# Cross network on one core: the searched run of row products is carried on to the row-major layer

## The chip, the cores and the metric

One core of a Trainium2 chip. The time is device microseconds (us) of one execution, median of several runs. A profile is one execution, in microseconds from the start of its span.

## What is computed

```
B, F, D, L = 16384, 26, 16, 6          # Din = F * D = 416
x = x0                                 # x0 [B, Din], ws [L, Din, Din], bs [L, Din], bf16
for l in range(L):
    proj = einsum('bd,de->be', x, ws[l]) + bs[l]
    x = x0 * proj + x
return x
```

## The kernel before

**Tiling.** The 16384 rows are eight groups g of 2048, and a job (g, l) is layer l of one group. All jobs but the last hold x transposed: features on partitions, rows along the free axis. 416 features are three blocks of 128 and a tail of 32. A tile (g, l, i) is the output block i of a job for its 2048 rows; it has four chunks j of 512 rows, and a chunk is one PSUM bank. A chunk sums 13 products over 32 input features each: 12 with `wm` (L1040) and one with the tail rows of the weights, `w3` (L1044). Such a row product uses one quarter of TensorE's rows, a strip, so four of them run side by side. Below, a *slot* is the time of one row product on each of the four strips. A chunk is 3.25 slots.

**The stream.** `stream` (L1005) emits most of the kernel's products. The order is a searched table, `ORDER`: each letter names a strip and how many chunks ago the chunk that it serves was begun, and stands for that chunk's 3 products on that strip, or 4 where the strip also holds its tail rows. The function `replay` turns letters into (time, strip, chunk, bank) by its own estimates; the instructions then go out in that order, with semaphores for what they really need. A bar `|` is an *event*: the strips stop and `tails` computes the 32 tail outputs of a batch of jobs, as 128x32 products (L697) and 32x32 corners (L685). Before, the stream runs from tile (0,2,1) to the tail rows of tile (7,4,0), with 14 events of three jobs.

**What follows a chunk.** ScalarE adds the bias and writes it from PSUM into `tw` (L550); for each pair of chunks VectorE multiplies by x0 (L562) and adds x (L567). Each add is held back until the next multiply is queued, or the tile ends. VectorE runs its instructions strictly in the order they were added. The tails of a batch go the same way with `ts`: the batch's job number 1 comes first, by VectorE straight from PSUM (L604), then the others by ScalarE (L608); multiply L610, add L612.

**Rotations.** For groups with `turn_of(g, 1)` above zero, the tail outputs of odd and even layers sit on different strips. `prefill`, called in `tails` when the batch is done, then copies the new tail of a job, rotated by some strips, into the buffer of the next tail: two DMAs on SyncE's queue (L444, L445). The add L612 of that job's *next* event adds into this buffer, so it waits for both DMAs. Groups 6 and 7 have such rotations.

**Outputs.** When the sixth layer of a group has its three tiles and its tail, `output(g)` puts on SyncE's queue a transpose of block 0 (L880), of the tail (L888), of blocks 1 and 2 (L880), and a store of the group (L916) that waits for them all. All go through one buffer `ost`. In `tails` this happens job by job in the batch's order, so the output of group 5, whose job (5,5) is the first of the 14th batch, stands on the queue ahead of the rotations of that batch's other two jobs.

**The end.** After the stream come, with whole 128-row products: (7,4,0) (L650), (6,5,0), (6,5,1), the last batch of tails (7,4) and (6,5), then (6,5,2) as 128x32 columns (L638), (7,4,1), (7,4,2), whose tail rows are L671 and L665. A job `FR` does whole products and then rows, `RF` the reverse, so that two jobs share one change of mode. The last job (7,5) is computed row-major for the output: for each kk of four, tail rows (L1171) and bias (L1176) by strips, whole products (L1130) into four banks, then ScalarE (L1182), VectorE multiply (L1188) and add (L1194), store (L1201). It needs x of (7,5), the outputs of the tiles (7,4,i), as weights (L1130, block by block) and row-major as `x5n`: block 0 and 1 by transposes on SyncE (`rest_turn`, L928), block 2 by TensorE (`turn_last`, L1141, copied by L1150), the tail by L1155 and L1163. The output of group 6 goes through `ost` as well; its transposes need the store of group 5 to have read `ost`.

Of the kernel before, what the change touches and what calls it, by code (L numbers as in the profile page):

```python
# [21 lines left out]
class Program:  # L22
# [182 lines left out]
    "ABCDAJCXaFTMWDUNSLYBKTMZjGANDaMpCPUJCXIROEDBaTUJCITVCQLVCAXNaALVaQHNKUTBQKDRICbRK|AJDWQJDCfUNSDM"  # L205
    "dSbJECbURCTINWDUJSPAJCTAZSPUJCDVYOTJAaDYVKTENCbNUSDJAXSYJGPAVODNUDOJUTCIRCDUNSbAJTaMVKHQBCXQNCPI"
    "ZSDJQCDMVaTEJOXBUDOAZXOIRGDYBSXARLOYBXKMZG|QBPSIVDCPAZOXQJGDQBaTINCLAdSXJYOHRACTNUCPJUSDAVCXRMaL"
    "FUCXARWPYBKPAdaLUNCLMVTCNISDcBWPIRCLAVSbMBKPYVSHMB|CTMVCPIVCDUNaTIBaTVAKTNUGDMVSDINCXYJCDMVSbIFW"
    "PQBCTMVCPIVSDIBWTANKTYVODAZOTUJGDURODINCbUJODBMSbIVCTUBSPIVGDQVCTMJWDAZSXINGDUBSXIBKTAZKPcRGAZPW"
    "QBP|QBOLRECTBCUPZSAPRaXASJPUBKUDVSAPRKAbSNcDOUbFKDURKDIRCbQJOXBIODVAOTUJCLQVCDUNSbEJWDQVCTINCbUJ"  # L210
    "ODIBaTVAKTNUGDMVSDINCXBcXSNAKPAZWLAVKTYNGDYNSDYN|ICXJTACVQPCNAPeVAPeRYLWNQDKNbCIBWTYBSLMVCLMVCXM"
    "JSDAdWPQBLOQBbKNQCDdMWTZEODNUKTABOXAVCTcVOLERCDcRaPAJWbMRKHYBCXQNCPIZSDJQCDMVaDMJSbAJTOYVGDMVCjU"
    "N|ISDJTAKRMDJCQDNeITVGMbBWIDRWIDRKAbJSMDBObQJCDdOQXJaMDJWMTBKAXhSMDJOUDVKQPFCMDBaQfVKALRWMDJOUDV"
    "KATBOYjREWDROULBKUTBSIBLCUdCMLZSAbJSUDRKMXeFLQBCXMR|CPISFDQCTIBaDUZKDQJWbMBXOIZCLQBSbIdODIVCTUJO"
    "DIVODIBbCNYXKERDCUdTaIBTaJUOHAVCTMVKDUJSDAVCXQNKDYJWfAJWTMZGDMVCXcNS|IDJTECRCTANaDYVKTMFWDUBOXAN"
    "KXZQODZATOJUCLURODINCbIBWTJYOHAVCTMVKDUJSDIRDCUNSbBISbVAKPURCLMRWDINCXIBWTJgOHAVCTMVKDUJSDAVCXQN"
    "KDYJSfAJaPURGDMdCbUN|ISDJTECRCTANaDMVKTFYWDAVOTYJGXAVODNUDOJUTCIRODIBSbUJPCIVDQCZTMBaLMBaXIBWLQZ"
    "ODIZCXQZKPAJWDRMWDNUKTBISBDUORbAOZDaULNQGXJCQXBAWPRaIDRKUDJSUPGBAbVCMDVOYLFSUPBeMXRCM|RCPISFDQCT"
    "IBaTIVOHQBPCMVDOAZWPBUOLQBCfURODIdWPQZGDQNCbINWDINXGQBPAWBQPKVDIVSPAJODYJCXQKZPEBWDQNWLAVKTAJSAD"
    "OVYDNKTYBKbMVSHBeMXRCM|RCPISFDQCDMVaTIBSbUBTKMVCLMVSDIBSXIZDKURDSMJCbIBSXIZOHQBCTMVCPIVSDQJCTIBa"  # L220
    "DUZSLAJbQOVHAOBbUOBLUChTIVOALVOQDJCXQBiLMSVDKMBbWJMHCVASXdIDJSUPCJUDSVIDSBMbRCMLRCcbJOALVMaDJMaD"
    "JYOXRAO|ANXKQBLSABOXYRGLMVDWNACbNQWDNISDJAWfBcSXJMGbVQCPRCPISFDAeTUBKTMVCLUNSDMJTCIBWTIdOHQBPCMV"
    "DOAZWPBUKDQVCfIRWPYFCXQZCPIRWDJQWPEBCTAZSPUJCLAZCXMRaLUBWLAVLSgNXGIRCDUNS|IDJTAKRMDJCQbJWATVCQPJ"
    "WALBaUTBODUadTIGVATVOIDJWAXRKYPFCMDBaMTCZMLRWALRCAfROUDJeUTaBQPKVEDVSMDJOAfJCQXKZMDJWATJWMDVKMTB"
    "CARaXMBKPZUDWRIPaAJbCYVTO|EJDWQBPCNAbOVLQCJDUiRLaAJbSUNDKMXCBMTWJYHOAVPCMVDOUBPWIRDIORXENKLAUKBN"
    "CD"
# [3 lines left out]
def replay(tails, events, needs, keep, part):  # L230
# [12 lines left out]
    size = [[(3 if c < n - keep else part) + (r == tails[c]) for r in range(4)] for c in range(n)]  # L243
# [62 lines left out]
def bass_standalone__cross_network_dcn__recsys_kernel(  # L306
# [21 lines left out]
    order[-6:] = [(5, 5), (7, 3), (6, 4), (7, 4), (6, 5), (7, 5)]  # L328
# [209 lines left out]
    def evacuate_chunk(g, l, i, j, b, read):  # L538
# [35 lines left out]
        if len(out_) == NJ:  # L574
            todo.append(lambda: finish_tile(g, l))
# [50 lines left out]
    HALVES = ((1, 2), (2, 1), (3, 0))  # L626
    halves = [63]

    def full(g, l, i, banks, first, chunk_major, after_chunk=None, chunks=range(NJ), ts_=range(NT), columns=False):
# [4 lines left out]
        for t, j in seq:  # L634
            if columns:
                for c in range(NJ):
                    o = slice(c * T32, (c + 1) * T32)
                    add("pe", lambda h, t=t, j=j, c=c, o=o: h.matmul(  # L638
                        psum[o, banks[j] * CH:(banks[j] + 1) * CH],
                        wm[l][:, t, i * P + c * T32:i * P + (c + 1) * T32], src(t, j, j + 1),  # L640
                        start=(first and t == 0), stop=(not first and t == NT - 1), tile_position=(0, c * T32)),
                        reads=[stok(t, j), wm_tok(l, i)], writes=[("ps", banks[j])])
                continue
            n = 1
            if (g, l) in HALVES and halves[0] and t != (0 if first else NT - 1):
                halves[0] -= 1
                n = 2
            w = CH // n
            for k in range(n):
                add("pe", lambda h, t=t, j=j, k=k, w=w: h.matmul(  # L650
                    bank(banks[j])[:, k * w:(k + 1) * w], wm[l][:, t, ecols], src(t, j, j + 1)[:, k * w:(k + 1) * w],
                    start=(first and t == 0), stop=(not first and t == NT - 1)),
                    reads=[stok(t, j), wm_tok(l, i)], writes=[("ps", banks[j])])
            if after_chunk and t == NT - 1:
                after_chunk(j)
# [21 lines left out]
    def tails(batch, corners_last=False, banks=None):  # L677
# [198 lines left out]
    def output(g):  # L876

        s, s3 = xset[(g, L)], xtail[(g, L)]
        def turn(t, j0=0, j1=NJ):
            add("sp", lambda h: h.dma_start_transpose(  # L880
                ost[:, j0 * KK:j1 * KK, t * P:(t + 1) * P], xs[s][:, t * GC + j0 * CH:t * GC + j1 * CH]),
                reads=[("x", s, t, j) for j in range(j0, j1)], writes=[("ost", t, j) for j in range(j0, j1)],
                lane="ot" if g < LAST - 1 else f"ot_{t}{j0}", batch=g)

        turn(0)
        if g == LAST - 1:
            turn(1)
        add("sp", lambda h: h.dma_start_transpose(ot3[:, :, :], x3s[s3][:, :]),  # L888
            reads=[("x3", s3)], writes=["ot3"], lane="ot3", batch=g)
        if g < LAST - 1:  # L890
            spread("pool")
# [3 lines left out]
        else:  # L895
            turn(2, 0, 2)
            turn(2, 2, NJ)
        free_x.append(s)
        free_3.append(s3)

# [35 lines left out]
    behind = ("tile", (LAST, L - 2), 0)  # L936
# [3 lines left out]
    tiles += [(jb, i) for jb in order[3:-1] for i in range(NT)]  # L940
# [4 lines left out]

    for i in range(1, NT):
        late = items.index(("tile", (LAST, L - 2), i))
        items.append(items.pop(late))
# [4 lines left out]
    while k < len(items):  # L953
# [8 lines left out]
        else:  # L962
            single = 1 if items[k] == behind else single + 1
# [25 lines left out]
    for n, it in enumerate(items):  # L989
        if it == behind:  # L990
            prev = None
# [11 lines left out]
    mode[len(items) - 1] = "RF"  # L1003

    def stream(run, keep, part):  # L1005
# [10 lines left out]
        needs = [[(t, place[(g, l - 1), t]) for t in range(NT if c < len(chunks) - keep else part)  # L1016
                  if c - place.get(((g, l - 1), t), -99) < 30] for c, ((g, l), i, j) in enumerate(chunks)]
        plan, read, left = replay([quad(g, l, j)[0] for (g, l), i, j in chunks], [len(b) for n, b in due],
                                  needs, keep, part)
# [4 lines left out]
        count, seen = {}, {}  # L1024
        for _, r, c, b in plan:
            if r < 0:
                dve[0] = max(dve[0], phases.pop(0)) + PAIR * len(behind_tail) + TAILS
                tails(due.pop(0)[1], corners_last=True, banks=c)
                continue
# [9 lines left out]
            if t < (NT if c < len(chunks) - keep else part):  # L1039
# [9 lines left out]
        home = {c: b for _, r, c, b in plan if r >= 0}  # L1049
        ring[:] = sorted(left)  # L1050
        (g, l), i, _ = chunks[-1]
        banks = [home[c] for c in range(len(chunks) - keep, len(chunks))]
        if (g, l + 1) not in xset:
            xset[(g, l + 1)] = free_x.pop(0)
# [22 lines left out]
    s_lo, s_hi = items.index(("tile", (0, 2), 1)), items.index(behind) + 1  # L1077
    for n, it in enumerate(items):
        if n == s_lo:
            stream(items[s_lo:s_hi], NJ, 0)  # L1080
        if s_lo <= n < s_hi - 1:
            continue
# [11 lines left out]
        if n == s_hi - 1:  # L1094
            pass
        elif mode[n] in ("FR", "F1"):
            banks = job_banks()
            full(g, l, i, banks, True, False, columns=items[n - 1][0] == "tails")
            rows32(g, l, i, banks, False, mode[n] == "F1")
            evacuate(g, l, i, banks, list(range(NJ)), 2)  # L1100
        else:
            banks = job_banks()
            rows32(g, l, i, banks, True)
            if n == len(items) - 1:
                full(g, l, i, banks, False, True, lambda j: evacuate(g, l, i, banks, [j], 1))
            else:
                full(g, l, i, banks, False, False)
                evacuate(g, l, i, banks, list(range(NJ)), 2)
        finish_tile(g, l)
        if (g, l) == (LAST, L - 2) and i < NT - 1:  # L1110
            if i:
                spread("act")
            rest_turn(i)


# [6 lines left out]

    def x3col(j, kk):
        return s3[quad(g, l, j)[1], kk * P:(kk + 1) * P]
# [43 lines left out]
    def nat_rows(kk, bks, first=True, begun=()):  # L1168
        for j in range(NJ):
            r, q = quad(g, l, j)  # L1170
            add("pe", lambda h, j=j, q=q, r=r: h.matmul(  # L1171
# [107 lines left out]
```

## Time and profile before

| what | us |
|---|---|
| median of 3 runs (lowest, highest) | 467.52 (467.04, 468.06) |
| span of the profiled execution, first to last instruction | 465.7 |
| what lies around the span, by the median | 1.8 |
| TensorE busy | 458.9 (99%) |
| VectorE busy | 404.2 (87%) |
| ScalarE busy | 379.1 (81%) |

The profiled execution's own time outside its span is not recorded, so the 1.8 us is the median less the span. The engines' busy shares are averages over stages with different limits; the stages at the end have to be read from the rows of the timeline. A row of the timeline has its start, its length, the engine (PE TensorE, DVE VectorE, ACT ScalarE, SPq SyncE's queue of DMAs), the line, the operation and its operands.

### The profile page before, as it was taken

Reading aid. Unit: us, or ns where it says so; the run is one execution under the profiler, and the core shown is the slowest. Engines: PE = TensorE matmul, PEld = TensorE weight load, DVE = VectorE, ACT = ScalarE, POOL = GpSimd, SP = SyncE. Lnnn points to the kernel's source line nnn. Section 1 sums busy time; section 2 is a strip of 40 time slices with the busy share of each in tenths; the row PEclk is TensorE's granted clock in tenths of the full one; section 3 lists DMA queues with packets and bytes.
Section 4 is the critical chain, followed back from the end, with each engine's and each line's share of the span. In section 5 each row is a group of like instructions: output and inputs, shape, how many; then the busy total and the mean of one; then the engine's idle time right before and its main releaser. Section 6 shows DMA issues by size and latency. Waiting matters only on the chain.

```text
span 465.7 us, 17469 instructions
## 1 busy us (share of the span) xinstructions
PE 458.9 (99%) x7827; PEld 263.8 (57%) x7833; DVE 404.2 (87%) x700; ACT 379.1 (81%) x608; POOL 6.8 (1%) x15
## 2 busy tenths in 40 slices
PE   9999999999999999999999999999999999999995
PEld 5444566555556677555655556565575566755442
DVE  2887998989989899979989898888989889898897
ACT  4687888788888888888878888788887887889785
POOL 1000000000000000000000000000000000000000
PEclk9999999999999999999999999999999999999998
DMA  8986949101002978084858437990100095027899
GB/s 229 185 177 144 160 113 190 29 3 26 1 4 38 158 210 155 22 141 149 149 92 154 145 78 141 160 296 23 25 2 4 25 148 172 14 49 169 183 161 292
DMA packets 139087, 53.77 MB, mean 115 GB/s; under 512 B 112762, under 2 KB 138500, under 8 KB 139012
## 3 DMA queue, kind: packets, MB, share of 16 engines
q1 hardware_dynamic: 138856, 52.54, 52.5%
q8 instruction: 61, 1.00, 0.9%
q10 hardware_dynamic: 156, 0.11, 0.1%
q14 instruction: 14, 0.11, 0.1%
HBM read 5.97 MB, written 13.63 MB: 42 GB/s over the span
## 4 chain that ended last, share of the span: by engine, by line
PE 93%; DVE 4%; DMA 1%; issue 1%; ACT 0%; SPq 0%; DVEq 0%
PE ps L1040 70%; PE ps L697 7%; PE ps L1044 6%; PE ps L650 6%; PE ps L638 2%; PE ps L685 1%; DMA wm<-in_ws_dram 1%; DVE x L1194 1%; DVE x L1188 1%; DVE x L528 1%; DVE tw L523 1%; PE ps L671 1%; ACT tw L514 0%; PE ps L789 0%; SPq L734 0%
## 5 line engine op out<-in xcount | busy, mean ns | idle before, releaser
L1040 PE MATMUL ps<-x,wm 32*128 32x512 bf16 x6000 | 356.0, 374 | 0.0
L550 ACT ACTIVATE tw<-ps,bias 128x512 bf16<-128x512 f32 x500 | 310.5, 688 | 46.4 <-PE ps L1040 35.9
L1040 PEld LDWEIGHTS ps<-x,wm 32*128 32x128 bf16 x6000 | 212.5, 92 | 127.7 <-ACT tw L550 4.1
L562 DVE TENSOR_TENSOR tw<-tw,x 128x1024 bf16<-128x1024 bf16 x250 | 168.2, 689 | 39.6 <-ACT tw L550 38.9
L567 DVE TENSOR_TENSOR x<-tw,x 128x1024 bf16<-128x1024 bf16 x250 | 163.5, 690 | 0.3
L1044 PE MATMUL ps<-x,w 32*128 32x512 bf16 x504 | 151.7, 374 | 0.0
L1044 PEld LDWEIGHTS ps<-x,w 32*128 32x128 bf16 x504 | 42.7, 92 | 6.6
L514 ACT ACTIVATE tw<-ps,bias 128x512 bf16<-128x512 f32 (+1 forms) x46 | 35.0, 839 | 12.0 <-PE ps L671 7.9
L650 PE MATMUL ps<-x,wm 128*128 128x512 bf16 x146 | 33.6, 379 | 1.0 <-issue 0.8
L697 PE MATMUL ps<-x,wm 128*32 128x512 bf16 x564 | 33.6, 380 | 0.0
L608 ACT ACTIVATE ts<-ps,bias 128x512 bf16<-128x512 f32 x33 | 21.0, 687 | 14.7 <-PE ps L685 14.7
L523 DVE TENSOR_TENSOR tw<-tw,x 128x1024 bf16<-128x1024 bf16 (+1 forms) x35 | 21.4, 627 | 4.9 <-ACT tw L514 4.7
L650 PEld LDWEIGHTS ps<-x,wm 128*128 128x128 bf16 x152 | 13.9, 98 | 19.0 <-issue 3.2
L697 PEld LDWEIGHTS ps<-x,wm 128*32 128x32 bf16 x564 | 13.5, 96 | 18.7 <-ACT tw L550 4.7
L528 DVE TENSOR_TENSOR x<-tw,x 128x1024 bf16<-128x1024 bf16 (+1 forms) x35 | 20.6, 624 | 0.0
L612 DVE TENSOR_TENSOR x<-ts,x 128x512 bf16<-128x512 bf16 x47 | 18.4, 420 | 0.4
L610 DVE TENSOR_TENSOR ts<-ts,x 128x512 bf16<-128x512 bf16 x33 | 13.0, 418 | 0.0
L604 DVE SCALAR_TENSOR_TENSOR ts<-ps,bias,x 128x512 bf16<-128x512 f32 x14 | 10.5, 748 | 2.2 <-PE ps L685 2.2
L909 POOL COPY ost<-ot 128x512 bf16<-128x512 bf16 x6 | 5.3, 890 | 411.3 <-DMA ot<-x 411.3
L1130 PE MATMUL ps<-wm,x 128*128 128x416 bf16 x48 | 9.8, 340 | 0.1
L1182 ACT ACTIVATE x<-ps 128x416 bf16<-128x416 f32 x16 | 7.6, 518 | 2.4 <-PE ps L1130 2.4
L799 DVE COPY x<-ps 128x512 bf16<-128x512 bf16 x5 | 2.0, 423 | 8.5 <-PE ps L789 8.5
(50 smaller groups left out, 76.9 us busy)
## 6 DMA issues: line engine op xcount, KB each, us to landing
out_dram<-ost SPq DMA_DIRECT2D x6, 1664.0 KB, 7.1
x<-x SPq DMA_DIRECT2D x24, 96.0 KB, 2.3
x<-in_x_dram SPq DMA_DIRECT2D x8, 208.0 KB, 4.4
x<-in_x_dram SPq DMA_DIRECT2D x4, 416.0 KB, 8.0
out_dram<-ost SPq DMA_DIRECT2D x2, 832.0 KB, 6.0
wm<-in_ws_dram SPq DMA_DIRECT2D x5, 312.0 KB, 3.4
x<-x SPq DMA_DIRECT2D x22, 64.0 KB, 2.0
out_dram<-x SPq DMA_DIRECT2D x3, 416.0 KB, 4.8
```

The source lines that it names most:

```text
L514: add("act", lambda h, a=a, w=w, b0=b0: h.activation(tw[r][:, a * CH:(a + w) * CH], psum[:, b0 * CH:(b0 + w) * CH], ACT_F.Identity, bias=b ...
L523: add("dve", lambda h, a=a, e=e: h.tensor_tensor(tw[r][:, a * CH:e * CH], tw[r][:, a * CH:e * CH], x0s[s0][:, i * GC + a * CH:i * GC + e * ...
L528: add("dve", lambda h, a=a, e=e: h.tensor_tensor(xs[so][:, i * GC + a * CH:i * GC + e * CH], tw[r][:, a * CH:e * CH], src(i, a, e), ALU.ad ...
L550: add("act", lambda h: h.activation(tw[r][:, j * CH:(j + 1) * CH], bank(b), ACT_F.Identity, bias=bias[:, i, l:l + 1], scale=1.0), reads=[( ...
L562: add("dve", lambda h: h.tensor_tensor(tw[r][:, o], tw[r][:, o], x0s[s0][:, c], ALU.mult), reads=[("tw", r, k) for k in both] + [x0_tok(s0 ...
L567: add("dve", lambda h: h.tensor_tensor(xs[so][:, c], tw[r][:, o], src(i, a, a + 2), ALU.add), reads=[("tw", r, k) for k in both] + [stok(i ...
L608: add("act", lambda h: h.activation(ts[r][:, :], bank(b), ACT_F.Identity, bias=bias[:, 3, l:l + 1], scale=1.0), reads=[("ps", b), "bias"], ...
L612: add("dve", lambda h: h.tensor_tensor(x3s[so][:, :], ts[r][:, :], res, ALU.add), reads=[("ts", r)] + rtok, writes=[("x3", so), ("x3", so, ...
L650: add("pe", lambda h, t=t, j=j, k=k, w=w: h.matmul(bank(banks[j])[:, k * w:(k + 1) * w], wm[l][:, t, ecols], src(t, j, j + 1)[:, k * w:(k ...
L697: add("pe", lambda h, t=t, j=j, src=src, l=l, b=b, ro=ro, qo=qo: h.matmul(psum[qo, b * CH:(b + 1) * CH], wm[l][:, t, NT * P:D], src(t, j, ...
L1040: add("pe", lambda h, l=l, t=t, j=j, b=b, q=q, ecols=ecols, src=src, kw=kw: h.matmul(bank(b), wm[l][q, t, ecols], src(t, j, j + 1)[q, :], ...
L1044: add("pe", lambda h, l=l, b=b, q=q, ecols=ecols, s3=s3, kw=kw: h.matmul(bank(b), w3[l][q, ecols], s3[q, :], **kw), reads=tok3 + [("w3", l ...
```

## The change

The stream runs to the last tile, (7,4,2), and has 15 events; its last four entries are the tail-row and bias products of the row-major layer's kk = 0 (two products for each chunk, on one strip). `stream` returns the banks of these four and the four free ones. The table `ORDER` is new from its first letter. The last jobs are reordered: (6,4) before (7,3), and the tiles of (6,5) and (7,4) are mixed. The 14th batch is now (5,5), (6,4), (7,3) and the 15th (6,5), (7,4). The whole products after the stream, the modes of the last items and `HALVES` go. The transposes of group 6's output are emitted tile by tile as its tiles finish, those of (7,4) likewise, and the transpose of group 6's tail with its batch.

```diff
-def replay(tails, events, needs, keep, part):
+def replay(tails, events, needs, keep):
-    size = [[(3 if c < n - keep else part) + (r == tails[c]) for r in range(4)] for c in range(n)]
+    size = [[3 + (r == tails[c]) if c < n - keep else 2 * (r == tails[c]) for r in range(4)] for c in range(n)]
...
-    order[-6:] = [(5, 5), (7, 3), (6, 4), (7, 4), (6, 5), (7, 5)]
+    order[-6:] = [(5, 5), (6, 4), (7, 3), (6, 5), (7, 4), (7, 5)]
...
         for g, l in batch:
+            if (g, l) == (LAST - 1, L - 1):
+                turn_rest(g)
             if corners_last:
                 prefill(g, l + 1)
...
+    def turn_rest(g):
+        s3 = xtail[(g, L)]
+        add("sp", lambda h: h.dma_start_transpose(ot3[:, :, :], x3s[s3][:, :]),
+            reads=[("x3", s3)], writes=["ot3"], lane="ot3", batch=g)
+
+    def turn_out(g, t):
+        s = xset[(g, L)]
+        for j0, j1 in ((0, NJ),) if t < NT - 1 else ((0, 2), (2, NJ)):
+            add("sp", lambda h, j0=j0, j1=j1: h.dma_start_transpose(
+                ost[:, j0 * KK:j1 * KK, t * P:(t + 1) * P], xs[s][:, t * GC + j0 * CH:t * GC + j1 * CH]),
+                reads=[("x", s, t, j) for j in range(j0, j1)], writes=[("ost", t, j) for j in range(j0, j1)],
+                lane=f"ot_{t}{j0}", batch=g)
...
-    tiles += [(jb, i) for jb in order[3:-1] for i in range(NT)]
+    tiles += [(jb, i) for jb in order[3:-3] for i in range(NT)]
+    end6, end7 = order[-3:-1]
+    tiles += [(end6, 0), (end6, 1), (end7, 0), (end6, 2), (end7, 1), (end7, 2)]
...
-    def finish_tile(g, l, n=1):
+    def finish_tile(g, l, n=1, i=0):
         tiles_done[(g, l)] = tiles_done.get((g, l), 0) + n
+        if (g, l) == (LAST - 1, L - 1):
+            turn_out(g, i)
+        elif (g, l) == (LAST, L - 2) and i < NT - 1:
+            if i:
+                spread("act")
+            rest_turn(i)
...
+    def nat_row(kk, j, b, first):
+        r, q = quad(LAST, L - 1, j)
+        s3, tok3 = x3_src(LAST, L - 1)
+        add("pe", lambda h: h.matmul(
+            bank(b, n=D), s3[q, kk * P:(kk + 1) * P], w3[L - 1][q, :], start=first, stop=False, tile_position=(r * T32, 0)),
+            reads=tok3 + [("w3", L - 1, r)], writes=[("ps", b)], row=r)
...
+            if c >= len(chunks):
+                j = c - len(chunks)
+                (nat_bias if j in natural else nat_row)(0, j, b, True)
+                natural[j] = b
+                continue
...
-        full(g, l, i, banks, False, True, lambda j: j % 2 and evacuate(g, l, i, banks, [j - 1, j], 2),
-             ts_=range(part, NT))
-        ring.extend(sorted(banks))
+        pr.flush()
+        return [natural[j] for j in range(NJ)], left
...
-    s_lo, s_hi = items.index(("tile", (0, 2), 1)), items.index(behind) + 1
+    s_lo = items.index(("tile", (0, 2), 1))
...
+    bka, left = stream(items[s_lo:])
...
     for j in range(NJ):
-        nat_full(0, j, bks[0][j], True, (0, 1))
+        nat_full(0, j, bks[0][j], False, (0, 1))
     turn_tails(b0)
-    nat_rows(0, bks[0], False)
     nat_full(1, 1, bks[1][1], True, (0, 1))
```

More of the change, by code (lines that the diff above doesn't have):

```diff
@@ L574, in evacuate_chunk @@
         if len(out_) == NJ:
[L575 removed]
+            todo.append(lambda: finish_tile(g, l, 1, i))
         while todo:
@@ L643, in full @@
                 continue
[L644 to L653, printed above, removed]
+            add("pe", lambda h, t=t, j=j: h.matmul(
+                bank(banks[j]), wm[l][:, t, ecols], src(t, j, j + 1),
+                start=(first and t == 0), stop=(not first and t == NT - 1)),
+                reads=[stok(t, j), wm_tok(l, i)], writes=[("ps", banks[j])])
             if after_chunk and t == NT - 1:
@@ L878, in output, with turn @@
         s, s3 = xset[(g, L)], xtail[(g, L)]
-        def turn(t, j0=0, j1=NJ):
+        def turn(t):
             add("sp", lambda h: h.dma_start_transpose(
[L881 to L889, printed above, removed]
+                ost[:, :, t * P:(t + 1) * P], xs[s][:, t * GC:(t + 1) * GC]),
+                reads=[("x", s, t, j) for j in range(NJ)], writes=[("ost", t, j) for j in range(NJ)],
+                lane="ot", batch=g)
         if g < LAST - 1:
+            turn(0)
+            turn_rest(g)
             spread("pool")
@@ L962, in bass_standalone__cross_network_dcn__recsys_kernel @@
         else:
-            single = 1 if items[k] == behind else single + 1
+            single += 1
         k += 1
```

125 lines of the change are left out of this document (46 added, 79 removed).

## The prediction

> **What bounds the kernel now.** I read the page first, then the chain of waits of the last 55 us, then the timeline there engine by engine. From the page, the chain by engine and the costliest group:
>
> ```profile
> PE 93%; DVE 4%; DMA 1%; issue 1%; ACT 0%; SPq 0%; DVEq 0%
> ...
> L1040 PE MATMUL ps<-x,wm 32*128 32x512 bf16 x6000 | 356.0, 374 | 0.0
> ```
>
> TensorE sets the pace, and the stream has no idle time of its own (last column 0.0). The chain of waits at the end (start, length, what):
>
> ```profile
> 413.77 2.06 PE ps L697 x36
> 415.83 0.35 PE ps L685 x12
> ...
> 429.67 2.54 PE ps L650 x11
> ...
> 438.40 1.41 PE ps L697 x24
> ...
> 442.78 2.27 ACT tw L514 x3
> ...
> 451.45 0.67 DVE x L528 x2
> ```
>
> An event of three jobs costs 2.06 + 0.35 = 2.41, one of two 1.41 + 0.35 = 1.76. From 442.78 on the chain runs through ScalarE and VectorE: the end waits for the last adds. SyncE's queue between the last two events, and the rotations' landings (the two L445 of that stretch):
>
> ```profile
> 418.54 1.83 SPq L888 DMA_TRANSPOSE ot<-x  x1
> 420.41 4.33 SPq L880 DMA_TRANSPOSE ost<-x  x2
> 427.55 0.41 SPq L916 DMA_DIRECT2D out_dram<-ost  x1
> 428.00 1.96 SPq L444 DMA_DIRECT2D x<-x  x1
> 430.37 1.00 SPq L445 DMA_DIRECT2D x<-x  x1
> 431.43 1.32 SPq L444 DMA_DIRECT2D x<-x  x1
> 432.80 0.59 SPq L445 DMA_DIRECT2D x<-x  x1
> ...
> 449.05 2.72 SPq L928 DMA_TRANSPOSE x<-x  x2
> ```
> ```profile
> L445 SPq DMA_DIRECT2D x<-x x2: 587/796/1005, 430.4 to 432.8; - x2
> ...
> DMA to landing us min/median/max: 2.9/3.9/4.9
> ```
>
> The rotations of the 14th event stand behind group 5's tail transpose, which waits for that event's tail (418.54), two more transposes and a store that waits for them (427.55). The last lands at 432.80 + 2.9 = 435.7, which is **19.5 us after the event ended** (415.83 + 0.35 = 416.18). VectorE's side:
>
> ```profile
> 416.42 0.74 DVE L604 SCALAR_TENSOR_TENSOR ts<-ps,bias,x 128x512 bf16<-128x512 f32 x1
> ...
> 443.14 0.76 DVE L612 TENSOR_TENSOR x<-ts,x 128x512 bf16<-128x512 bf16 x2
> ...
> 451.37 0.75 DVE L528 TENSOR_TENSOR x<-tw,x 128x512 bf16<-128x512 bf16 x2
> ...
> 454.39 1.08 DVE L1194 TENSOR_TENSOR x<-x,x 128x832 bf16<-128x832 bf16 x2
> ```
>
> The adds that need the rotated tails run at 443.14, 7.4 us after the landing: now the rotations are hidden.
>
> **The change, part by part.** All is priced to the end of the stream, then to the end of the kernel.
>
> *TensorE.* I count the letters: 1626 slots before, 1569.75 of them up to the end of the 14th event; 1705 after (77 more for the rest of the last six tiles, and 2 for the tail and bias rows of the row-major layer). From 40.74 (the first L1040) to 416.18 there are 375.4 us; less 14 x 2.41 = 33.7, over 1569.75 slots, 0.2176 us a slot with all edges. After: 1705 x 0.2176 = 371.0, + 33.7, + 1.76, from 40.74: 447.2. Draining at the end costs something: before, the last 56.25 slots took 416.18 to 429.5 = 13.3 against 12.2, 1.1 lost. Here row-major rows fill the gaps of two strips; between 0 and 1.1 I take 0.4: **the stream ends at 447.6**. Before, the row-major products began at 448.50, and their first tail and bias rows (450.46 to 450.92, 0.46) still came. If nothing else bound, that is a gain of 0.9 to 1.4. The new table may be looser or denser elsewhere; 0.2 us for each of 15 sections is what edges cost now, so I allow 1 us either way. `HALVES` costs nothing: its jobs are all in the stream already, no product is split.
>
> *The two last events.* In the new table the 14th event stands at slot 1596.5, 26.75 later than before: it ends at 416.18 + 26.75 x 0.2176 = 422.0. The 15th follows after only 61 letters, 49.75 slots, 10.8 us: from 432.8 to 434.6. Before it began 21.6 us after the 14th's end (437.8). The batch still begins with (5,5), so group 5's output is still ahead of the rotations of (6,4)'s and (7,3)'s new tails on SyncE's queue, and nothing in that row of DMAs gets shorter. The rotations land at 422.0 + 19.5 = **441.5**. The adds L612 of the 15th event need them, and would be due at 434.6 + 0.2 + two or three short instructions (0.74 + 0.4) = 435.9. So **VectorE stands for some 5.6 us**, and everything queued behind it: the pairs of five tiles.
>
> *Does the wait reach the end?* ScalarE is not held: the four `tw` buffers that the last tiles take were left by tiles finished before the wait, or (for (7,4,2)) by (6,5,1), finished by 444.6. So TensorE's stream goes on, and ends at 447.6 as above. VectorE's account from 441.5: two adds of tails 0.7, then five tiles (6,5,1), (7,4,0), (6,5,2), (7,4,1), (7,4,2), each four instructions of 0.604 (two L562 in a row take 1.29, the second ends 0.69 after its start, so 0.60 each) = 2.42. That is 442.2 + 12.1 = **454.3** for the last add, all inputs having long come. Before it was 451.37 + 0.67 = 452.0: **2.3 later**. Without the wait, the same account with pairs coming as the letters let them has about 1.9 us of idle time in it and the last add near 451.1, 1.0 earlier.
> The row-major layer: its products with block 1 can start on (7,4,1), at 451.3 for the first half against 448.75 before; the transposes on TensorE of block 2 at 453.7 against 451.28. Both 2.4 to 2.6 late. From there nothing changed.
>
> *SyncE.* The transposes of group 6 and of (7,4) follow their tiles' adds: the last pair (L928) comes after (7,4,1), at 451.4, against 449.05: 2.4 late too, and no worse, as its queue is drained by then (group 5's store lands 6.8 after its issue, 440.1).
>
> *Sum.* 465.7 + 2.4 = 468.1 of span; with the 1.8 around it **469.9, say 470.0**. The bounds of the rotation's landing: the first of these DMAs took 1.96 to issue and its landing followed the store's; had they behaved as the median ones (0.58 to issue, 2.0 to land) the last would land at 416.18 + 14.2 = 430.4, shifted 436.2, and the wait would be next to nothing. Upwards, 1.5 later by the spread of the two landings (2.9 to 4.9). I take the row itself, since the store ahead of them is the same: 441.5. VectorE's lateness goes one to one into the end while it exceeds its idle 1.9.
>
> **A second price, the clock.** While VectorE catches up, TensorE has nothing to do from 447.8 to 451.3, 3.5 us. The granted clock near the end (last number but two of each row is PEclk):
>
> ```profile
> 462.00:463.00 1.00, 0.00 (x0) 0.00 (x0) 0.41 (x2) 0.00 (x0) 0.00 (x0) 1.00 1.12 332
> 463.00:464.00 1.00, 0.00 (x0) 0.00 (x0) 0.00 (x0) 0.00 (x0) 0.00 (x0) 0.60 1.11 330
> 464.00:465.00 1.00, 0.00 (x0) 0.00 (x0) 0.00 (x0) 0.00 (x0) 0.00 (x0) 0.50 0.18 50
> ```
>
> The last product ends at 460.7 and the clock halves at about 463.2, after 2.5 us. An idle time of 3.5 us could do the same in mid-work. How long it stays low no row shows; between nothing and the whole rest (9.4 us of products, doubled), I take as long as it took to drop, 2.5 us at half speed, a loss of 1.3: 471.3. [...]
>
> **The rivals.**
> 1. *The wait as above, clock kept*: 470.0 (469.0 to 471.0). For it: the queue order and the 19.5 us. Chance 0.46.
> 2. *The wait and a dropped clock*: 471.3 (470.8 to 472.6). Chance 0.27.
> 3. *The other side: the rotations are in time.* One mechanism: the L444 and L445 of the 14th event find a free queue and land by 437.5; from there up the wait only uses VectorE's idle 1.9. Then the gain of the stream counts: the block-2 transposes on TensorE start 0.8 earlier, 466.7. For it: rotations elsewhere land 2.0 after issue. Against: these wait behind a store that waits for transposes. Chance 0.16.
> 4. *Rotations in time, but SyncE's queue is the bound*: group 6's first transpose waits for the store of group 5 (440.1), then eight transposes of 1.3 to 1.9, 12.6 us, end at 452.7 against 449.05 + 2.72 = 451.8: 0.9 late at the add L1194, 468.0. Chance 0.11.
>
> **How the numbers follow.** A measurement here can tell about 0.2%, 0.9 us, from no change. Case 1 is the likeliest: 470.0. Slower by more holds for cases 1 and 2 but for a little of 1's lower edge, and some of 4: 0.76. Faster by more (below 466.6) needs case 3 with a denser table: 0.12. Within: 0.12. The range reaches from case 3's better half's edge, 467.0, to 472.4, which takes in the clock's price; case 1's own is 469.0 to 471.0.
>
> **What would show it.** In the changed profile: L612 of the 15th event waiting some 5 us on a DMA `x<-x`, VectorE idle near 436 to 441 and with no gap from there to the last add; the last event's corner products at 434; the row-major products (L1130 before) with an idle time of about 3.5 us ended by VectorE; the granted clock below 1.00 after it, or not (case 2). I am wrong if VectorE has no such gap, or the stream ends well off 447.6, or the rotations land before 437.5.

## The result, and the profile after

| | before | after |
|---|---|---|
| median, us (lowest, highest) | 467.49 (467.04, 468.06) | 472.39 (472.14, 473.11) |
| span of the profiled execution | 465.7 | 470.3 |
| first product of the stream to first whole row-major product | 407.8 | 406.9 |
| first to last whole row-major product | 11.9 | 17.0 |
| group 6's store issued | 451.95 | 457.42 |
| last add ends | 462.40 | 466.89 |

The ratio is 1.0107, 95% interval 1.0093 to 1.0121: slower, by 4.9 us where 2.5 was forecast. The stream did become shorter, by 0.84 us (third row of the table; its end comes 1.28 us earlier in the span, as it also begins 0.44 earlier), and more than that was lost behind it (the fourth).

From the page of the kernel after, the chain by engine and three groups (busy time, mean ns of one, idle time before them and its releaser):

```profile
PE 88%; DVE 5%; DMA 3%; SPq 2%; issue 0%; ACT 0%; DVEq 0%; ACTq 0%
...
L1061 PE MATMUL ps<-x,wm 32*128 32x512 bf16 x6288 | 372.4, 374 | 0.0
...
L613 DVE TENSOR_TENSOR x<-ts,x 128x512 bf16<-128x512 bf16 x47 | 18.5, 420 | 5.4 <-DMA x<-x 5.0
...
L1126 PE MATMUL ps<-wm,x 128*128 128x416 bf16 x48 | 11.0, 371 | 4.5 <-DVE x L568 4.5
```

L613 is the former L612 and L1126 the former L1130. The stream (L1061, before L1040) still has no idle time. Two waits that matter are new: VectorE for a DMA, and TensorE for VectorE. A third, of ScalarE, comes below. The timeline of VectorE after shows the first in its place (in brackets the idle time ahead of the row):

```profile
441.12 0.42 DVE L613 TENSOR_TENSOR x<-ts,x 128x512 bf16<-128x512 bf16 x1 [5.03 <-DMA x<-x]
441.47 0.69 DVE L568 TENSOR_TENSOR x<-tw,x 128x1024 bf16<-128x1024 bf16 x1
```

The chain of waits after runs from SyncE's queue through that wait to the last adds:

```profile
428.07 4.40 DMA ost<-x
...
438.06 2.97 DMA x<-x
...
451.38 0.61 DVE x L568
...
452.03 2.61 PE ps L1126 x7
...
455.91 3.44 DMA x<-x
...
459.44 0.59 DVE x L1184
```

Up to 452.03 it is the chain that the prediction drew. Two pieces it didn't have: seven products that take 2.61 us (at full clock seven take 1.41, below), and at 455.91 a DMA that the second add of the row-major layer waits for. That DMA is the last pair of transposes on SyncE's queue, whose timeline after is:

```profile
432.49 0.41 SPq L917 DMA_DIRECT2D out_dram<-ost  x1
...
442.18 2.24 SPq L897 DMA_TRANSPOSE ost<-x  x1
...
454.54 2.71 SPq L929 DMA_TRANSPOSE x<-x  x2
457.42 1.14 SPq L917 DMA_DIRECT2D out_dram<-ost  x2
```

The store of group 6 goes out at 457.42. Before, it was 451.95, and the same queue read:

```profile
435.23 1.81 SPq L928 DMA_TRANSPOSE x<-x  x1
438.85 5.67 SPq L880 DMA_TRANSPOSE ost<-x  x2
444.57 1.69 SPq L888 DMA_TRANSPOSE ot<-x  x1
...
451.95 1.87 SPq L916 DMA_DIRECT2D out_dram<-ost  x2
```

At that store SyncE's queue is 5.5 us late, more than VectorE is (its last add of (7,4,2) ends at 454.99 against 452.12). The transposes begin at 442.18 because the add that finishes (6,5,0) is the L568 of 441.47 above: it is queued right behind the waiting L613 and ends at 442.16. One wait has two exits, one through VectorE and TensorE, one through SyncE. From 442.18 to 457.25 SyncE issues eight transposes back to back, 15.1 us.

ScalarE waits too, for the second of these transposes: its `spread` (L908, which reads the transposed tail of group 6) stands in its queue ahead of the bias adds of (7,4,2).

```profile
449.35 0.63 ACT L908 ACTIVATE ost<-ot 128x512 bf16<-128x512 bf16 x1 [2.88 <-DMA ot<-x]
449.89 2.41 ACT L551 ACTIVATE tw<-ps,bias 128x512 bf16<-128x512 f32 x4
```

Here it costs nothing: the bias adds end at 452.30, and VectorE comes to these pairs at 452.50. In some of the runs below it does cost.

The windows of the kernel after (last three numbers of a row: granted clock, busy share of the DMA engines, GB/s):

```profile
451.00:452.00 1.00, 0.00 (x0) 0.00 (x0) 1.00 (x3) 1.00 (x3) 0.00 (x0) 0.66 1.13 213
452.00:453.00 1.00, 0.97 (x3) 0.44 (x4) 1.00 (x2) 0.29 (x1) 0.00 (x0) 0.50 1.11 207
...
454.00:455.00 1.00, 1.00 (x8) 0.64 (x7) 0.99 (x2) 0.00 (x0) 0.00 (x0) 0.63 0.93 180
...
467.00:468.00 1.00, 0.00 (x0) 0.00 (x0) 0.00 (x0) 0.00 (x0) 0.00 (x0) 1.00 1.11 333
```

TensorE's idle time halves the clock, from 451.3 to 454.7 by the shares 0.66 and 0.63 (a window that is at 1.00 for its first 0.32 us and at 0.50 for the rest has the mean 0.66). And the last microseconds are full of stores: from 459 to 468 the rate is 331 to 337 GB/s in every window, with the DMA engines busy throughout, though the last add ended at 466.89. The chain of waits says nothing of them: it ends with that add, 3.4 us before the end of the span.

### The profile page after: what moved, and what is told of

It is laid out like the page before. It is cut to its first block, busy times and chain, and to the rows that moved or that the text cites. A ratio compares the mean times of both kernels' runs of the same rounds, so it can differ in the third digit from the quotient of the medians.

```text
span 470.3 us, 17809 instructions
## 1 busy us (share of the span) xinstructions
PE 459.2 (98%) x8001; PEld 263.9 (56%) x8001; DVE 403.6 (86%) x696; ACT 381.2 (81%) x609; POOL 5.9 (1%) x15
## 3 DMA queue, kind: packets, MB, share of 16 engines
q8 instruction: 62, 1.02, 0.9%
## 4 chain that ended last, share of the span: by engine, by line
PE 88%; DVE 5%; DMA 3%; SPq 2%; issue 0%; ACT 0%; DVEq 0%; ACTq 0%
PE ps L1061 68%; PE ps L689 6%; PE ps L1065 6%; PE ps L642 4%; DMA x<-x 1%; DVE tw L563 1%; DVE x L568 1%; PE ps L636 1%; PE ps L677 1%; DMA ost<-x 1%; DMA x<-in_x_dram 1%; DVE x L1184 1%; SPq L445 1%; DVE x L1178 1%; SPq L874 1%; PE ps L1126 1%
## 5 line engine op out<-in xcount | busy, mean ns | idle before, releaser
L1061 PE MATMUL ps<-x,wm 32*128 32x512 bf16 x6288 | 372.4, 374 | 0.0
L551 ACT ACTIVATE tw<-ps,bias 128x512 bf16<-128x512 f32 x524 | 326.5, 688 | 50.0 <-PE ps L1061 39.4
L1061 PEld LDWEIGHTS ps<-x,wm 32*128 32x128 bf16 x6288 | 220.3, 92 | 136.5 <-ACT tw L551 6.3
L563 DVE TENSOR_TENSOR tw<-tw,x 128x1024 bf16<-128x1024 bf16 x262 | 176.4, 689 | 41.0 <-ACT tw L551 39.9
L568 DVE TENSOR_TENSOR x<-tw,x 128x1024 bf16<-128x1024 bf16 x262 | 171.2, 689 | 0.3
L1065 PE MATMUL ps<-x,w 32*128 32x512 bf16 x524 | 158.1, 374 | 0.0
L515 ACT ACTIVATE tw<-ps,bias 128x1024 bf16<-128x1024 f32 (+1 forms) x24 | 20.7, 938 | 8.1 <-PE ps L663 7.0
L613 DVE TENSOR_TENSOR x<-ts,x 128x512 bf16<-128x512 bf16 x47 | 18.5, 420 | 5.4 <-DMA x<-x 5.0
L642 PE MATMUL ps<-x,wm 128*128 128x512 bf16 x92 | 21.3, 380 | 0.1
L1126 PE MATMUL ps<-wm,x 128*128 128x416 bf16 x48 | 11.0, 371 | 4.5 <-DVE x L568 4.5
L524 DVE TENSOR_TENSOR tw<-tw,x 128x1024 bf16<-128x1024 bf16 (+1 forms) x21 | 13.0, 637 | 2.2 <-ACT tw L515 2.1
L611 DVE TENSOR_TENSOR ts<-ts,x 128x512 bf16<-128x512 bf16 x32 | 12.7, 419 | 0.0
L529 DVE TENSOR_TENSOR x<-tw,x 128x1024 bf16<-128x1024 bf16 (+1 forms) x21 | 12.6, 634 | 0.0
L1126 PEld LDWEIGHTS ps<-wm,x 128*128 128x128 bf16 x48 | 4.5, 104 | 9.4 <-DVE x L568 5.3
```

The lines of the kernel that those rows point to most:

```text
L515: add("act", lambda h, a=a, w=w, b0=b0: h.activation(tw[r][:, a * CH:(a + w) * CH], psum[:, b0 * CH:(b0 + w) * CH], ACT_F.Identity, bias=b ...
L524: add("dve", lambda h, a=a, e=e: h.tensor_tensor(tw[r][:, a * CH:e * CH], tw[r][:, a * CH:e * CH], x0s[s0][:, i * GC + a * CH:i * GC + e * ...
L551: add("act", lambda h: h.activation(tw[r][:, j * CH:(j + 1) * CH], bank(b), ACT_F.Identity, bias=bias[:, i, l:l + 1], scale=1.0), reads=[( ...
L563: add("dve", lambda h: h.tensor_tensor(tw[r][:, o], tw[r][:, o], x0s[s0][:, c], ALU.mult), reads=[("tw", r, k) for k in both] + [x0_tok(s0 ...
L568: add("dve", lambda h: h.tensor_tensor(xs[so][:, c], tw[r][:, o], src(i, a, a + 2), ALU.add), reads=[("tw", r, k) for k in both] + [stok(i ...
L613: add("dve", lambda h: h.tensor_tensor(x3s[so][:, :], ts[r][:, :], res, ALU.add), reads=[("ts", r)] + rtok, writes=[("x3", so), ("x3", so, ...
```

## The experiments

Each is a version of the kernel after with one or more edits, timed beside the kernel before. "Store" is the issue of group 6's store in the profiled execution.

| run | median (lowest, highest) | ratio, interval | store | last add ends | span |
|---|---|---|---|---|---|
| rot_first | 476.06 (475.81, 476.94) | 1.0182, 1.0169 to 1.0195 | 461.57 | 470.89 | 474.3 |
| rot_pool | 470.93 (470.59, 472.62) | 1.0078, 1.0064 to 1.0092 | 458.00 | 467.73 | 470.8 |
| spread_rot | 470.92 (470.83, 471.39) | 1.0073, 1.0060 to 1.0086 | 456.37 | 465.72 | 469.0 |
| x5_first | 473.21 (472.51, 473.65) | 1.0121, 1.0106 to 1.0135 | 458.09 | 467.83 | 470.7 |
| warm_x5 | 475.05 (472.58, 475.63) | 1.0149, 1.0131 to 1.0168 | 458.90 | 471.46 | 473.7 |
| x5s | 473.19 (472.59, 474.24) | 1.0116, 1.0101 to 1.0131 | 459.38 | 468.28 | 471.9 |
| x5s_warm | 472.61 (471.88, 473.96) | 1.0104, 1.0090 to 1.0118 | 458.31 | 465.69 | 470.8 |
| bar15_36 | 474.08 (472.90, 474.39) | 1.0124, 1.0109 to 1.0140 | 456.66 | 470.32 | 472.6 |
| no_out5 | 468.40 (467.67, 469.01) | 1.0015, 1.0007 to 1.0024 | 453.76 | 463.05 | 466.5 |
| b14_28 | 468.95 (468.28, 470.75) | 1.0034, 1.0021 to 1.0047 | 454.42 | 463.75 | 467.2 |
| turns | 469.63 (467.90, 470.11) | 1.0037, 1.0025 to 1.0049 | 453.35 | 462.63 | 466.1 |
| b14_all | 470.25 (468.81, 470.63) | 1.0048, 1.0036 to 1.0060 | 454.23 | 463.52 | 467.0 |
| b14_x5s | 470.29 (469.69, 470.92) | 1.0052, 1.0039 to 1.0065 | 455.31 | 462.59 | 467.9 |
| b14_x5s_no6 | 466.79 (466.10, 468.08) | 0.9983, 0.9975 to 0.9992 | none | 462.04 | 464.3 |

A profile is one execution. Those of turns, b14_all, b14_x5s, b14_x5s_no6, spread_rot, x5_first and the kernel after are of the fastest execution of theirs, those of rot_pool and bar15_36 of the slowest; medians are compared by the ratios.

### Is it the wait for the rotations?

**rot_first** issues the four rotation DMAs of the 14th event ahead of group 5's output.

```diff
+        early = batch[0] == (5, 5)
+        if early:
+            for g, l in batch:
+                prefill(g, l + 1)
         for g, l in batch:
...
-            if corners_last:
+            if early:
+                filled.add((g, l + 1))
+            elif corners_last:
                 prefill(g, l + 1)
```

> The changed kernel with the rotations of the 14th event (L445, L446) queued ahead of group 5's output instead of behind it. Theory A (two limits in a row: VectorE's wait for the rotations, and behind it SyncE's queue, whose eight transposes of the last two groups can start only when group 5's store has read ost and then run back to back for 15 us): the 5.0 us wait of L613 is gone, but group 5's output is 2.4 us later, so the chain of transposes still starts near 442.3 and ends near 457, the second add L1184 near 459.3: 471 to 472.4 us. Theory B (VectorE's wait for the rotations is the whole loss, the slower clock follows from it): both go, 466.7 us.

It came out slower than the kernel after, outside both expectations. VectorE no longer waits at L613, but it waits later. Its timeline in rot_first:

```profile
454.06 0.69 DVE L563 TENSOR_TENSOR tw<-tw,x 128x1024 bf16<-128x1024 bf16 x1 [5.20 <-ACT tw L551]
```

and SyncE's:

```profile
438.19 0.41 SPq L923 DMA_DIRECT2D out_dram<-ost  x1
446.68 2.95 SPq L903 DMA_TRANSPOSE ost<-x  x1
449.68 1.26 SPq L897 DMA_TRANSPOSE ot<-x  x1
```

Group 5's output went out 5.7 us later than in the kernel after, where its block 0 was transposed as early as 407.36; now that transpose, too, stands behind the rotations (425.87). So `ost` came free late. The first transpose of group 6 now waits for `ost`, 8.5 us after the issue of the store, although (6,5,0) was finished at 437.5. Its tail transpose follows. ScalarE has the `spread` of that tail (which reads the transposed tail) in its queue ahead of the bias adds of (7,4,2), and so VectorE waits. The reuse of `ost` and the order on ScalarE's queue were in neither theory.

**rot_pool** puts the same four DMAs on GpSimd's queue instead, so that neither output nor rotations wait for each other.

```diff
...
+        eng = "pool" if batch in ((6, 5), (7, 4)) else "sp"
+        lane = f"rotp{batch[0]}" if eng == "pool" else lane
-        add("sp", lambda h: h.dma_start(dst[n * T32:P, :], src[0:a, :]), reads=reads, writes=[token], lane=lane, batch=batch)
+        add(eng, lambda h: h.dma_start(dst[n * T32:P, :], src[0:a, :]), reads=reads, writes=[token], lane=lane, batch=batch)
...
```

(A first line, not shown, keeps these DMAs out of the order that the other GpSimd instructions keep among themselves.)

> The changed kernel with the same four rotation DMAs issued by GpSimd's queue. Theory A: the wait of L613 is gone and SyncE's queue is free of 5.7 us of rotations behind group 5's store, so the transposes start when that store has landed, at 439.9 instead of 442.2: 2.3 us less than the changed kernel, 470.1 us. Theory B: 466.7 us.

A's side, 470.9 against its 470.1. Without the wait at L613 some 1.4 us of the 4.9 come back (1.0107 to 1.0078), no more: `ost` still sets the transposes (store of group 5 at 434.77, 2.3 later than in the kernel after, where A had left it; first transpose of group 6 at 442.33), and `spread` still holds ScalarE, for whose bias adds VectorE then stands 2.63 us (L565 at 451.44).

**spread_rot** takes that away too: it is rot_pool with `spread` after (7,4,2)'s bias adds.

```diff
-            if i:
-                spread("act")
             rest_turn(i)
...
+    spread("act")
     store(LAST - 1, 0, 2)
```

> rot_pool with ScalarE's spread of group 6's tail queued after the bias adds of (7,4,2) instead of ahead of them. ScalarE's wait for the tail transpose goes, VectorE's last add comes near 450.7, TensorE doesn't stand still. Theory A: L931 still stands last on SyncE's queue, issued at 455.1 and 456.5, so the second add L1184 is at 459.8 as in rot_pool, 470.9 us. Theory E (ScalarE's spread is the limit once the rotations are out of the way): 467 us.

A again: no gain in the median over rot_pool (1.0078, now 1.0073). VectorE is on time, and stands at the end for SyncE's queue, for the pairs of x row-major (L929). VectorE's timeline in spread_rot:

```profile
457.07 0.59 DVE L1184 TENSOR_TENSOR x<-x,x 128x832 bf16<-128x832 bf16 x1 [3.49 <-DMA x<-x]
458.27 0.59 DVE L1184 TENSOR_TENSOR x<-x,x 128x832 bf16<-128x832 bf16 x1 [0.61 <-DMA x<-x]
```

The multiply ahead of it was done at 453.6. So SyncE's queue alone, with VectorE on time, costs 3.4 us (0.0073 of 467.6).

**bar15_36** moves the bar of the 15th event 36 letters (29.5 slots) later instead, so that the rotations are in time for it; only the table differs.

> The changed kernel with the bar of the 15th event 36 letters (29.5 slots, 6.4 us) later, so that it ends after the rotations have landed; the 14th event stays. Theory A (the lateness of group 5's output limits the end also through ost and SyncE's queue): the wait of L613 is gone, but the transposes still run from 442 to 457 and the time stays within 1 us of 472.4. Theory B (the gap between the two events is the whole cause): 467 us.

474.1: not B's, and 1.7 above 472.4, more than the 1 that A allowed. The transposes do run from 441.10 to 456.49, as A said. L613 doesn't wait, but the tail of (6,5) is later, so its transpose is, and `spread` holds ScalarE and with it TensorE. ScalarE's timeline in bar15_36:

```profile
452.33 0.63 ACT L908 ACTIVATE ost<-ot 128x512 bf16<-128x512 bf16 x1 [5.22 <-DMA ot<-x]
```

### The order on SyncE's queue, and the clock

**x5_first** puts the last pair L929, of (7,4,1), ahead of group 6's block 2 on SyncE's queue.

```diff
         if (g, l) == (LAST - 1, L - 1):
-            turn_out(g, i)
+            if i < NT - 1:
+                turn_out(g, i)
...
             rest_turn(i)
+            if i:
+                turn_out(LAST - 1, NT - 1)
```

> The changed kernel with the two half transposes of block 1 of (7,4) (L929) queued ahead of the two of group 6's block 2 (L897). Theory A: L929 is issued at 452.0 and 453.4 instead of 454.5 and 455.9 and lands by 458.2; the second add L1184 then waits for the row-major products on a halved clock instead, 0.6 earlier: 471.8 us. Theory B: SyncE's queue doesn't matter, 472.4 us.

No gain, and 0.8 above B's number; the interval overlaps with that of the kernel after. The second add no longer waits, but the store of group 6 went from 457.42 to 458.09: a first hint that the store counts.

**warm_x5** is x5_first with 14 products of constants into TensorE's idle time, which compute nothing that is used.

> x5_first, and 14 whole products of constants into a free bank in TensorE's idle time behind the stream (3.0 us of 4.5), whose results nothing reads. Theory A: the clock stays full, the first add L1184 comes 1.3 earlier, the second when L929 has landed, 458.2: 471.2 us. Theory C (the halved clock alone sets the end behind the wait): 470.9 us here, and no change from x5_first alone.

A miss, and its own fault: the bank that they write was held by ScalarE until 452.6, the products ran slowly (14 in 5.92 us; at a clock of 1.00, in x5s_warm below, 14 take 3.23) and pushed the row-major layer to 458.4. It says nothing of either theory. It was made again with a free bank: **x5s** is x5_first with the late `spread`, and **x5s_warm** adds 15 products of constants into a bank that is free.

```diff
+    keep_busy(60, b0)
     for j in range(NJ):
         nat_full(0, j, bks[0][j], False, (0, 1))
```

> x5_first with the late spread; the 14th event where the changed kernel has it, the rotations behind group 5's output. Control of the next run. VectorE still waits 5 us for the rotations, TensorE still stands 4.5 us, the clock halves: 473.2 us as x5_first.

> x5s with 15 whole products of constants (3.2 us) into the first bank that ScalarE frees, in TensorE's idle time. Their results are not read. If the halved clock costs what the slow products show (2.61 for 7 instead of 1.40, the transposes 1.06 instead of 0.61), the clock stays at 1.00 from 447 to 457 and the time falls by 1.5 to 2 us against x5s, to 471.5 us. If the clock is no limit, no change.

TensorE's timeline in x5s_warm:

```profile
447.82 3.23 PE L765 MATMUL ps<-const-bfloat16-1.0 128*128 128x512 bf16 x14 [0.16 <-issue]
...
452.16 1.41 PE L1127 MATMUL ps<-wm,x 128*128 128x416 bf16 x7 [0.93 <-DVE x L568]
```

The clock is 1.00 in every window until the end, and the seven products take 1.41 instead of 2.61. The last add ends 2.6 us earlier than in x5s (465.69 against 468.28). Of that, 1.1 is not the clock: in the profile of x5s the rotations land later, and L613 runs at 442.35 against 441.25. The other 1.5 is: in x5s the copy behind the transposes on TensorE waits 1.60 us for them, here not at all. The median falls by only 0.6, and the intervals overlap. So the clock costs 1.5 us at the last add, but the last add doesn't set the end. Group 6's store seems to: it is issued 1.07 us earlier in this profile than in x5s, and the span is 1.1 shorter. b14_x5s_no6 below shows it.

### Group 5's output earlier

**no_out5** leaves the output of group 5 out.

```diff
-        if g < LAST - 1:
+        if g < LAST - 2:
             turn(0)
```

> The changed kernel without the output of group 5: its four transposes, its spread and its store are left out. Theory A (everything late at the end, the rotations, ost, and through SyncE's queue the tail transpose that ScalarE's spread waits for, is late because group 5's output begins 5.8 us later on one queue): the wait of L613 goes, the spread on ScalarE doesn't wait, the second add L1184 comes near 454, 466.4 us. Theory D (the new table makes TensorE's or VectorE's end later by itself): above 468 us.

By the time D's side: 0.7 us slower than before. The wait at L613 and the low clock are gone, yet the eight transposes run from 437.97 to 453.57, and the second add waits 0.30 us for the last. This is what remains when nothing comes before them. It was not tested apart, but the rows offer a reason: before, the first transpose of (7,4) stood ahead of them (issued at 435.23, L928) in a time in which the queue was free; now it stands among them.

**b14_28** moves the bar of the 14th event 28 letters (23 slots) earlier, so that group 5's output and the rotations are earlier.

> The changed kernel with the bar of the 14th event moved 28 letters (23 slots, 5.0 us) earlier in the table, nothing else; the gap to the 15th is then 72.75 slots. Theory A: group 5's store is issued at 427.5, has read ost by 435, the rotations land at 436.6, 1 us after L613 is due, which VectorE's idle time takes in; the end is the stream's: 466.6 us. Theory D: no better than 471 us.

A's direction, 2.3 above its number. L613 waits 0.45 us, the transposes start at 438.91, TensorE has its clock. The stream is 0.5 longer (407.4).

**turns** leaves the table alone and queues group 5's transposes of blocks 1 and 2, which are ready, ahead of its tail's.

```diff
             turn(0)
+            if g == 5:
+                turn(1)
+                turn(2)
             turn_rest(g)
             spread("pool")
-            turn(1)
-            turn(2)
+            if g < 5:
+                turn(1)
+                turn(2)
             store(g, 0, NJ)
```

> The changed kernel, its table untouched; of group 5's output the transposes of blocks 1 and 2 are queued ahead of the tail's transpose, so they run before the 14th event's tail is there. Theory A (the late output of group 5 is the cause, through the rotations and through ost): its store is issued at 428.7 instead of 432.5, the rotations land at 437.3 instead of 441.0, the wait of L613 falls to 1.3 us, SyncE's eight transposes start at 437.5 and the store of group 6 is issued at 453; the end follows that store by 12.6 us and the last add by 3.4: 466.5 us of span, 468.3 us. If the new table itself makes the end late, no better than 471 us.

SyncE's timeline in turns:

```profile
427.17 0.41 SPq L921 DMA_DIRECT2D out_dram<-ost  x1
...
437.44 2.34 SPq L901 DMA_TRANSPOSE ost<-x  x1
...
453.35 1.14 SPq L921 DMA_DIRECT2D out_dram<-ost  x2
```

The store of group 5 goes 5.3 us earlier than in the kernel after, with not one product moved, and about two thirds of the loss are gone (1.0107 to 1.0037). A said 468.3, the median is 469.63; executions lie from 467.9 to 470.1, and the profile is of the fastest. The profile's store is still 1.4 later than before.

**b14_all** joins b14_28, rot_pool and the late `spread`; **b14_x5s** joins b14_28, the late `spread` and L929 first.

> b14_28, with the rotations on GpSimd's queue and the late spread. Theory A: what little was left of the waits goes, 466.2 us, 0.2 to 0.5 below b14_28. Theory D: no better than 470 us.

> b14_28 with the late spread and with the halves of block 1 of (7,4) (L929) ahead of group 6's block 2 on SyncE's queue. Theory A: the second add L1184 no longer waits for L929 (it waited 0.61 in b14_28), the row-major part takes 12.3 us from its first to its last whole product as in spread_rot, and the end follows it by 5.2: about 465.6 of span, 467.2 us, 1.5 below b14_28 and level with the kernel before. Theory D (b14_28 is limited elsewhere): 468.9 us.

Both missed, by 4.1 and 3.1, and neither beats b14_28. In b14_x5s the last add ends at 462.59, as before (462.40), and yet the span is 467.9, 2.2 longer. One of its windows after the last add:

```profile
464.00:465.00 1.00, 0.00 (x0) 0.00 (x0) 0.00 (x0) 0.00 (x0) 0.00 (x0) 0.51 1.10 335
```

No engine works there, and the stores run at 335 GB/s. **b14_x5s_no6** is that kernel without group 6's store.

```diff
-    store(LAST - 1, 0, 2)
-    store(LAST - 1, 2, NJ)
```

> b14_x5s without the store of group 6's output, which is left out. Theory F (in b14_x5s the last add is at 462.6, but the end is set by 3.3 MB of stores written at 332 GB/s from the issue of group 6's store on): the end follows the last add by 3.4 us again, 466.0 us of span instead of 467.9, 468.0 us or less. If the stores don't matter: as b14_x5s, 470.2 us.

Theory F: the span falls to 464.3, by 3.6, with the last add only 0.55 earlier, and the median by 3.5. The span is 1.7 below F's own 466.0, as the end follows the last add by 2.3 and not by 3.4. Two of its windows show that no stores are queued up any more:

```profile
457.00:458.00 1.00, 1.00 (x12) 0.31 (x10) 0.96 (x3) 0.98 (x3) 0.00 (x0) 1.00 0.39 123
460.00:461.00 1.00, 0.37 (x3) 0.00 (x0) 0.97 (x3) 0.91 (x2) 0.00 (x0) 1.00 0.42 141
```

So **the store of group 6 sets the end** of b14_x5s. Groups 6 and 7 are 2 x 2048 x 416 x 2 bytes = 3.41 MB; at the 332 GB/s of the windows that is 10.3 us, and it can't begin before group 6's store is issued. The table has the two bounds side by side. The span ends 12.5 to 12.8 us after that store in eleven of the thirteen runs that have it, while it ends 2.9 to 5.3 after the last add there. In warm_x5 and bar15_36, where TensorE was late and slow (14 products in 5.92 us; a clock of 0.50 from 452 to 460), it ends 2.2 and 2.3 after the last add, as in b14_x5s_no6 (2.3): that is what the last add costs when no stores are queued ahead.

By these two numbers the kernel after ends by its stores: 457.42 + 12.8 = 470.2, measured 470.3, while its last add alone would give 466.89 + 2.3 = 469.2. The other exit, through TensorE, lies 1.1 us below. For the kernel before, both numbers give less than its 465.7: 464.8 by the store and 464.7 by the last add. That it ends by its stores, too, is argued from its windows alone, which show 330 to 368 GB/s in every one from 454 to 464:

```profile
453.00:454.00 1.00, 1.00 (x13) 0.42 (x13) 1.00 (x3) 0.85 (x3) 0.00 (x0) 1.00 0.57 124
454.00:455.00 1.00, 1.00 (x7) 0.56 (x6) 1.00 (x3) 0.82 (x3) 0.00 (x0) 1.00 1.11 368
```

## Why the prediction was right and wrong

**The stream.** Forecast to end at 447.6; the first whole row-major product starts at 447.22. Right; the gain is 1.28 in the span, within the 0.9 to 1.4, of which 0.44 is the earlier start of the stream.

**The rotations.** 15th event at 432.8, measured 432.23; rotations landed at 441.5, measured 441.03; VectorE stands 5.6 us, measured 5.03. Right, down to the line and the releaser.

**VectorE's account.** Last add of (7,4,2) at 454.3, measured 454.99. The five tiles take 12.1, as forecast. Too small was the "two adds of tails 0.7": between the two adds stand an L568 and an L611, and from 441.12 to the first multiply it is 1.74. The end before was 452.12 and not 452.0, so the adds are 2.87 late. "ScalarE is not held" was wrong: the `spread` holds it for 2.88, without cost here.

**The clock.** Case 2 was what happened, and it had the smaller chance. The loss on the path is 1.01: the first add of the row-major layer is 3.88 late (458.27 against 454.39), VectorE's adds 2.87. Most of it is VectorE's wait for the slow transposes on TensorE:

```profile
455.81 1.49 DVE L1146 COPY x<-ps 128x1024 bf16<-128x1024 bf16 x2 [0.82 <-PE ps L1137]
```

The 1.01 is less than the 1.3 priced. The clock fell 3.8 us after the last product, not 2.5, and stayed low for 3.4, where the prediction had 2.5 as its author's estimate. Why it falls when it does, and stays low as long as it does, no run shows.

**The step that failed** is SyncE's: "2.4 late too, and no worse, as its queue is drained by then". The pair L929 was put at 451.4; it was issued at 454.54. I dated a row of eight transposes by the last of them, when each of them waits for the one ahead, and the first can't start before (6,5,0)'s add, at 442.16, behind the very wait that I had found. Rival 4 had that row, with 12.6 us for it, but only for the case that the rotations are in time; it took 15.1. And so "From there nothing changed" failed: the second add waits 0.59 for that pair, and the store of group 6, which no step of the prediction prices, went out at 457.42 where it had been 451.95, 5.5 us late and not 2.4.

**What bounds the end** was misread before that: "the end waits for the last adds" is what the chain of waits shows. It is not so in the kernel after, nor, as far as its windows show, in the kernel before. The chain follows instructions, and ends at the last add; the windows behind it, at over 330 GB/s, were in the prediction's own fence, read for their clock alone.

**The sum.** Forecast 2.4 late. By the last add it is 4.5: 2.87 from VectorE's queue, 1.01 from the clock, 0.59 from the last pair. By what sets the end it is 5.5 for the issue of group 6's store, less 0.9 because the end follows sooner (before, 13.7 us pass from that issue to the end, after 12.9; the rate reaches 330 GB/s 2.0 us after the issue before, and 1.3 after): 4.6 of span. In the kernel after both run through the wait that was forecast, and so the direction was right; its exit through SyncE is the larger, and was priced at nothing of its own. But the wait is not the cause of all: without it, in rot_pool and spread_rot, the store still goes out at 458.00 and 456.37, behind the late `ost`. What lies under both is the late output of group 5, as turns and b14_28 show. Rival 3's 466.7 was out of reach for the same store: with the rotations in time or nearly so, it is issued at 453.4 or 454.4 (turns, b14_28), still later than before.

**What stays open.** Without group 5's output, 0.7 us of the loss remain (no_out5), and no run took the new order of the last tiles apart to find them. What of turns' remaining 1.7 us (1.0037) is the later first transpose of (7,4) and what is the spread of its executions wasn't separated. A second `ost` buffer, and group 6's output stored in smaller pieces, weren't tried. No version that writes the whole output beat the kernel before.

## What to carry to other kernels

Price every queue that issues DMAs as a list in order, from its first late entry to the last store, with the buffers that it reuses. When the last microseconds are full of stores, count the end also from the issue of the first of them (here it came 12.5 to 12.8 us later in eleven of thirteen runs, 10.3 of that for the bytes at 332 GB/s), whatever the chain of waits says: in b14_x5s the last add was as early as before and the span 2.2 us longer, because that store went out 3.4 later. When one wait is found, look for what else is queued behind the instruction that waits: here one L613 delayed TensorE through one neighbour and SyncE through the next.

## What the runs showed of the hardware

- Four copies of 32 to 96 KB from SBUF to SBUF, issued behind a store of 1.7 MB, took 2.43, 1.02, 1.16 and 0.60 us to issue in the kernel after; with no store ahead, in rot_first, the same four took 0.54 to 0.60 each.
- Stores of the output reach 331 to 337 GB/s in the last windows of the kernel after (459 to 468), with the DMA engines' share at 1.10 to 1.12.
- The halved clock lasted 3.4 us in the kernel after and 6.8 in x5s, by the shares of their windows. In bar15_36 it was at 0.97 from 450 to 452 and at 0.50 in every window from 452 to 460, and ten products begun at 460.67 took 2.63 us instead of 1.93: from these, an estimate of 10.2 us. It fell 3.8 us after the last product in the kernel after, 2.5 before and 2.0 in x5s and bar15_36, so in these runs no fixed idle time sets the moment.
- Products of constants into a free bank, 14 of them recorded in 3.23 us, kept the clock at 1.00 in every window of x5s_warm from 444 to 460, where x5s has it at 0.50 from 450.7 to 457.6; begun after 5.65 us of idle time, in warm_x5, 14 took 5.92 us.
